# Three x tiles instead of two transposed on TensorE in the first stage of a gated mix of linear attention and GEGLU

## Chip, cores and metric

One core of one Trainium2 chip runs the kernel. The metric is the device time of one execution in microseconds (us), lower is better. A trace records one execution; its span, from the first instruction to the last, is about 1.25 us shorter than the time of the same execution.

## The reference

```python
# x: [1, 2048, 640]; 32 heads of 20; F = 1728; all bf16
g = sigmoid((x * gate_w).sum(-1, keepdims=True))
q, k, v = split(x @ wqkv)                          # [2048, 640] each
phi = lambda t: where(t > 0, t + 1, exp(t)) + 1e-6
kv  = einsum("bhsd,bhse->bhde", phi(k), v);  z = phi(k).sum over s
a   = (phi(q) @ kv) / (phi(q) . z + 1e-6) @ wo
b   = (gelu(x @ w_gate) * (x @ w_up)) @ w_down
out = g * a + (1 - g) * b
```

## The kernel before

The 2048 rows of x are 16 tiles of 128. For each tile, TensorE needs x transposed (five blocks of 128x128, one for each 128-row chunk `k` of the weights), multiplies it with the key and query columns of `wqkv`, and ScalarE and VectorE turn the sums in PSUM (the memory that TensorE's results go to, used here as eight banks, 0 to 7) into `phi(k)` and `phi(q)` ("phi" below). Loads are started on two queues, SP's and ACT's; a load "lands" when its data is there for the engines. Tiles 2 to 15 get their transpose from DMA and go through a per-tile loop, `KQ`. Tiles 0 and 1 are loaded plainly and transposed on TensorE, because that data is there sooner; they make up the first stage, which the change is about. In it, key products are made chunk by chunk as the chunks of the key weights land.

```python
NXN = 2                                   # tiles transposed on TensorE
load_x(0)                                 # SP queue unless "act" is given
load_wk(0)
load_x(1, "act")
load_wk(1)
load_wk(3)
load_wk(2, "act")
load_wk(4, "act")
# ... gate_w on ACT ...
load_wq(0, 2)                             # query weights, chunks 0-1
load_wq(2, KC, "act")                     # chunks 2-4
for i in range(NXN, NT):                  # DMA transposes, behind key chunk 4
    load_xT(i, after=([r_wk[4]] if i == NXN else ()))
# ...
SLOTS = [(0, 1), (2, 3), (4, 5), (6, 7)]  # PSUM banks of the n-th entry
seq = [("k", 0), ("k", 1), ("q", 0), ("q", 1)]
# KM(n, ks): key products of entry n, chunks ks;  QM(n, ks): query products
# T(i, ks, bank): transposes of tile i, then VectorE copies them to SBUF
# warm(count, n): filler matmuls of n columns on constants
warm(5, 512)
warm(1, 128)
T(0, [0], 7); T(0, [1, 2, 3, 4], 6)
warm(6, 128)
KM(0, [0])
T(1, [0], 7); T(1, [1, 2, 3, 4], 6)
warm(3, 128)
KM(1, [0])
for k in (1, 3):
    KM(0, [k]); KM(1, [k])
gate_col()
for k in (2, 4):
    KM(0, [k]); KM(1, [k])
# ... phi of the keys; QM of tiles 0 and 1 by chunk; phi of the queries ...
def KQ(i):
    b = 3 * (i % 2)                       # banks 0-2 or 3-5
    # ... 5 x (512 + 512 + 257 columns), then phi ...
for i in range(2, NT):
    KQ(i)
MGROUP = [((3, 4), (6, 7)), ((0, 1, 2), (3, 4, 5))]   # banks of the next stage
```

## Time and profile before

| | before |
|---|---|
| time, median of the first 3 runs (lowest to highest) | 274.45 us (274.27 to 275.06) |
| span of the trace | 273.2 us |
| TensorE busy | 269.7 us, 99% |
| first key matmul | 4.62 us |
| start of the per-tile loop (tile 2) | 11.40 us |
| from there to the start of the last matmul | 259.64 us |

The first part of the page of before: engine, busy time, share of the span, instructions.

```profile
PE 269.7 (99%) x1369; PEld 128.6 (47%) x1369; DVE 141.9 (52%) x251; ACT 76.0 (28%) x132; POOL 30.0 (11%) x28
```

TensorE (PE) is the limit. From 11.40 us on it has no gap of note, so the change can win only in the first 11 us. The timeline of PE there, for before; the columns are start, duration, engine, line of the kernel, operation, operands, count, and in brackets the idle time before and what ended it. L453 and L454 are one key chunk of one tile (512 and 128 columns), L433 the transposes, L419 the fillers, L540 the per-tile loop.

```profile
4.62 0.38 PE L453 MATMUL ps<-pool 128*128 128x512 bf16 x1 [0.18 <-DMA pool<-in_A_wqkv_dram]
4.84 0.22 PE L454 MATMUL ps<-pool 128*128 128x128 bf16 x1
4.89 0.44 PE L433 MATMUL ps<-pool 128*128 128x128 bf16 x5
5.17 0.34 PE L419 MATMUL ps<-const-bfloat16-1.0 128*128 128x128 bf16 x3
5.43 0.39 PE L453 MATMUL ps<-pool 128*128 128x512 bf16 x1
...
6.20 0.22 PE L454 MATMUL ps<-pool 128*128 128x128 bf16 x1
7.01 0.39 PE L453 MATMUL ps<-pool 128*128 128x512 bf16 x1 [0.59 <-DMA pool<-in_A_wqkv_dram]
...
11.40 0.38 PE L540 MATMUL ps<-pool 128*128 128x512 bf16 x1
```

Matmuls overlap, so the work is counted from start to start: 4.62 to 4.84 to 4.89 is 0.27 us for one key chunk of one tile; five transposes take 4.89 to 5.17, 0.28 us. After the matmul at 6.20 us TensorE stands still until key chunk 3 lands: 0.59 us after its modelled end, and 0.76 us more from start to start than without the wait. That is what the change goes for. The windows view of before, in the same stretch, ends with the DMA share and the rate:

```profile
core 0: us, PE busy (x) PEld busy (x) DVE busy (x) ACT busy (x) POOL busy (x), PEclk, DMA share, GB/s
5.00:6.00 1.00, 1.00 (x14) 0.67 (x12) 0.65 (x2) 0.00 (x0) 0.00 (x0) 1.00 1.02 302
6.00:7.00 1.00, 0.42 (x4) 0.08 (x2) 0.00 (x0) 0.00 (x0) 0.00 (x0) 1.00 0.94 308
```

The DMA engines are about full while TensorE waits (0.94 to 1.02), so I took it that in this trace the data could come in another order, but hardly sooner in total. The Trainium skill ("DMA: Bandwidth & Descriptors", Issuing engines are not separate DMA queues) says that copies issued by either engine run on the same 16 DMA engines and interleave. The landings agree: on SP, key chunks 0, 1 and 3 landed at 4.49, 5.46 and 6.96 us; on ACT, tile 1 of x and key chunks 2 and 4 at 4.68, 5.68 and 7.16. The column PEclk, the granted clock, reads 1.00 here.

### The profile page before, as it was taken

To read this page: it belongs to the slowest core of one execution; us is meant where nothing else is said; L and a number is where in the kernel's file an instruction comes from. 1 tells how busy PE (TensorE), PEld (TensorE's weight loads), DVE (VectorE), ACT (ScalarE), POOL (GpSimd) and SP (SyncE) were. 2 spreads that over 40 slices of the span, in tenths; PEclk is the share of its full clock that TensorE was granted. 3 is DMA by queue.
4 is the path that set the end of the run, shared out by engine and by line. 5 is a ranking of instruction groups with operands and counts; after the bars stand their busy time and mean duration, and the time that the engine had idled before them with its cause. 6 is when DMAs were issued, how large, how long until landed. Compare 5 with 4: busy or idle time off the path is not lost.

```text
span 273.2 us, 3449 instructions
## 1 busy us (share of the span) xinstructions
PE 269.7 (99%) x1369; PEld 128.6 (47%) x1369; DVE 141.9 (52%) x251; ACT 76.0 (28%) x132; POOL 30.0 (11%) x28
## 2 busy tenths in 40 slices
PE   7999999999999999999999999999999999999997
PEld 4555555544445444444444444444444444444444
DVE  2588989998234334999999999634210000000200
ACT  2355555310421454223222223224011121121021
POOL 5000000003240001242332422000000000000000
PEclk9999999999999999999999999999999999999999
DMA  6675999500300011522121221263031110110211
GB/s 207 179 118 122 322 402 386 143 3 12 65 19 2 23 49 51 182 45 48 26 48 24 48 42 34 60 215 109 5 77 38 41 38 19 38 41 19 58 58 41
DMA packets 42160, 23.61 MB, mean 86 GB/s; under 512 B 31519, under 2 KB 40735, under 8 KB 42015
## 3 DMA queue, kind: packets, MB, share of 16 engines
q1 hardware_dynamic: 41269, 22.40, 30.0%
q10 hardware_dynamic: 874, 0.98, 1.0%
q8 instruction: 11, 0.18, 0.3%
q14 instruction: 6, 0.05, 0.0%
HBM read 13.83 MB, written 2.63 MB: 60 GB/s over the span
## 4 chain that ended last, share of the span: by engine, by line
PE 97%; DMA 2%; SPq 0%; DVE 0%; issue 0%
PE ps L701 41%; PE ps L865 23%; PE ps L540 14%; PE ps L597 6%; PE ps L844 4%; DMA pool<-in_A_wqkv_dram 2%; PE ps L679 2%; PE ps L812 2%; PE ps L600 1%; PE ps L468 1%; PE ps L825 1%; PE ps L453 1%; PE ps L722 1%; PE ps L740 0%; SPq L340 0%; PE ps L469 0%
## 5 line engine op out<-in xcount | busy, mean ns | idle before, releaser
L701 PE MATMUL ps<-pool 128*128 128x512 bf16 x520 | 113.7, 379 | 0.0
L701 PEld LDWEIGHTS ps<-pool 128*128 128x128 bf16 x520 | 50.5, 98 | 60.0
L865 PE MATMUL ps<-pool 128*128 128x512 bf16 (+2 forms) x306 | 62.7, 367 | 0.0
L707 ACT ACTIVATE pool<-ps 128x512 f32<-128x512 f32 x52 | 31.0, 597 | 73.1 <-PE ps L701 73.1
L709 DVE TENSOR_TENSOR pool<-ps,pool 128x512 bf16<-128x512 f32 x52 | 34.7, 689 | 31.7 <-PE ps L701 30.4
L865 PEld LDWEIGHTS ps<-pool 128*128 128x128 bf16 x306 | 29.2, 98 | 33.4 <-issue 0.4
L540 PE MATMUL ps<-pool 128*128 128x512 bf16 (+1 forms) x210 | 38.1, 344 | 0.0
L848 DVE TENSOR_TENSOR pool<-ps,pool 128x512 bf16<-128x512 f32 x4 | 2.8, 692 | 61.5 <-PE ps L844 61.5
L755 POOL TENSOR_TENSOR pool<-pool 128x640 f32<-128x640 bf16 x16 | 22.5, 1406 | 72.9 <-DVE pool L757 66.2
L872 ACT ACTIVATE pool<-ps,pool 128x512 bf16<-128x512 f32 (+1 forms) x16 | 10.9, 681 | 68.6 <-PE ps L865 68.6
L540 PEld LDWEIGHTS ps<-pool 128*128 128x128 bf16 x210 | 20.5, 98 | 17.5
L559 DVE SCALAR_TENSOR_TENSOR pool<-ps,pool 128x128 bf16<-128x128 f32 (+2 forms) x42 | 25.3, 602 | 2.4
L550 ACT ACTIVATE pool<-ps 128x640 bf16<-128x640 f32 x28 | 19.7, 704 | 18.2 <-DVE pool L559 10.9
L597 PE MATMUL ps<-pool 128*128 128x512 bf16 x78 | 19.4, 379 | 0.0
L765 DVE TENSOR_TENSOR pool<-pool 128x640 bf16<-128x640 bf16 x16 | 13.2, 826 | 0.6
L763 DVE TENSOR_SCALAR pool<-pool 128x32 f32<-128x32 f32 x16 | 12.8, 802 | 0.6
L757 DVE TENSOR_REDUCE pool<-pool 128x32 f32<-128x640 f32 x16 | 12.9, 807 | 0.0
L645 DVE TENSOR_TENSOR pool<-pool 128x640 f32<-128x640 f32 x14 | 11.6, 825 | 0.5
L844 PE MATMUL ps<-pool 128*128 128x512 bf16 x52 | 11.6, 379 | 0.0
L647 POOL PARTITION_ALL_REDUCE pool<-pool x1 | 4.0, 3972 | 61.5 <-DVE pool L645 61.5
L597 PEld LDWEIGHTS ps<-pool 128*128 128x128 bf16 x78 | 7.0, 98 | 7.3
L556 DVE TENSOR_SCALAR pool<-pool 128x640 bf16<-128x640 bf16 x28 | 9.2, 327 | 1.8 <-ACT pool L550 0.3
(70 smaller groups left out, 105.8 us busy)
## 6 DMA issues: line engine op xcount, KB each, us to landing
out_dram<-pool SPq DMA_DIRECT2D x19, 128.0 KB, 1.7
pool<-in_B_w_gate_dram SPq DMA_DIRECT2D x1, 2080.0 KB, 13.8
pool<-in_B_w_up_dram SPq DMA_DIRECT2D x1, 2080.0 KB, 19.3
pool<-in_A_x_dram SPq DMA_DIRECT2D x1, 1280.0 KB, 8.6
pool<-in_B_w_down_dram SPq DMA_DIRECT2D x1, 1120.0 KB, 6.0
pool<-omg_row SPq DMA_DIRECT2D x1, 1024.0 KB, 4.8
pool<-in_A_x_dram SPq DMA_DIRECT2D x1, 960.0 KB, 5.7
pool<-in_A_wo_dram SPq DMA_DIRECT2D x6, 160.0 KB, 10.0
```

Of the source, the lines that this page charges most:

```text
L540: last = e.matmul(ps[:, b + p, 0:c1 - c0], xT[:, k, i * 128:(i + 1) * 128], wkq[:, k, c0:c1], start=(k == 0), stop=(k == KC - 1))
L550: P.op("act", lambda e: e.activation(e_buf[m], ps_flat[:, o:o + 640], ACT.Exp), reads=banks, writes=[r_e[m]])
L559: P.op("dve", lambda e, c0=c0, c1=c1: e.scalar_tensor_tensor(dst[:, c0:c1], ps_flat[:, o + c0:o + c1], 1.0 + EPS, e_buf[m][:, c0:c1], ALU. ...
L597: last = e.matmul(ps[:, b, :], pk[i][:, c * 128:(c + 1) * 128], x_aug[:, i, 0:512], start=(i == 0), stop=(i == NT - 1))
L701: last = e.matmul(ps[:, b, :], w[:, k, fc * 128:(fc + 1) * 128], xT[:, k, j * 512:(j + 1) * 512], start=(k == 0), stop=(k == KC - 1))
L707: P.op("act", lambda e: e.activation(ge[n], ps[:, gb, :], ACT.Gelu_apprx_tanh), reads=[bank[gb]], writes=[r_ge[n]])
L709: P.op("dve", lambda e: e.tensor_tensor(hT[fc][:, j * 512:(j + 1) * 512], ps[:, ub, :], ge[n], ALU.mult), reads=[bank[ub], r_ge[n]], write ...
L755: P.op("pool", lambda e: e.tensor_tensor(tmp[n], pq[i], z_b, ALU.mult), reads=[r_pq[i], r_zb], writes=[r_tmp[n]])
L757: P.op("dve", lambda e: e.tensor_reduce(den[n], tmp[n].rearrange("p (h d) -> p h d", h=32), AX.X, ALU.add), reads=[r_tmp[n]], writes=[r_de ...
L765: P.op("dve", lambda e: e.tensor_tensor(pq[i].rearrange("p (h d) -> p h d", h=32), pq[i].rearrange("p (h d) -> p h d", h=32), den[n].unsqu ...
L844: last = e.matmul(ps[:, b, :], wd[:, fc, 512:640], hT[fc][:, j * 512:(j + 1) * 512], start=False, stop=(fc == NFC - 2), skip_group_check=True)
L865: last = e.matmul(ps[:, pb, 0:c1 - c0], lhs, rhs, start=False, stop=(q == len(rows) - 1), skip_group_check=True)
```

## The change

The intent: while the key chunks land, give TensorE a third tile to work on, so that it has 0.81 us of work for each landed chunk instead of 0.54, and fill the wait. Tile 2 is loaded plainly, ahead of key chunk 2; keys of three tiles are made by chunk, then queries tile by tile. Six accumulations now share the four pairs of banks, so the queries of tiles 1 and 2 reuse the banks of the keys of tiles 0 and 1. The banks of the loop and of the next stage are shifted to fit.

```diff
-NXN = 2
+NXN = 3
@@ loads @@
+            load_wk(4)
+            load_x(2, "act")
             load_wk(2, "act")
-            load_wk(4, "act")
-            load_wq(0, 2)
-            load_wq(2, KC, "act")
+            for k in range(KC):
+                load_wq(k, ("act", "sp")[k % 2])
@@ first stage @@
-            seq = [("k", 0), ("k", 1), ("q", 0), ("q", 1)]
+            seq = [("k", 0), ("k", 1), ("k", 2), ("q", 0), ("q", 1), ("q", 2)]
             KM(1, [0])
-            (chunks 1, 3, gate, 2, 4 of tiles 0 and 1; phi; queries of both by chunk)
+            KM(0, [1])
+            KM(1, [1])
+            T(2, [0], 7)
+            T(2, [1, 2, 3, 4], 6)
+            KM(0, [2])
+            KM(1, [2])
+            for k in range(3):
+                KM(2, [k])
+            for n in range(3):
+                KM(n, [3])
             gate_col()
+            for n in range(3):
+                KM(n, [4])
+            for n in range(3):
+                phi1(n)
+                phi2(n)
+            for n in range(3, 6):
+                for k in range(KC):
+                    QM(n, [k])
+                phi1(n)
+                phi2(n)
@@ banks @@
-                b = 3 * (i % 2)
+                b = 4 * (i % 2)
-            for i in range(2, NT):
+            for i in range(NXN, NT):
-            MGROUP = [((3, 4), (6, 7)), ((0, 1, 2), (3, 4, 5))]
+            MGROUP = [((3, 4), (3, 7)), ((0, 1, 2), (4, 5, 6))]
```

(The first removed line in brackets stands for the old loop; the bulk load of x starts one tile later, by NXN.)

## The prediction

> # Prediction
>
> **What bounds the kernel now.** TensorE: the page's first part gives PE 269.7 us busy of a 273.2 us span (99%); the chain of waits is 97% PE. From 11.40 us (start of the per-tile stage, in the timeline) to the end the chain is matmuls without a gap, the granted clock 1.000. Only the first 11 us can give anything. There the timeline shows real matmuls from 4.62 us (key chunk 0 landed), a hole of 0.59 us before 7.01 us that ends on a wqkv DMA (key chunk 3, issued at 2.21 on SP, landing 4.8 us later), then dense work. The DMA engines are 0.8 to 1.08 busy from 2 to 8 us (the windows view). The Trainium skill ("DMA: Bandwidth & Descriptors", Issuing engines are not separate DMA queues) says that copies started by either engine run on the same 16 DMA engines and interleave; the trace agrees: the 160 KB key chunks 0 to 4, issued on SP and ACT, land at about 4.6, 5.4, 5.7, 7.0 and 7.1 us.
>
> **What the change does.** The projection work stays: 5 x 0.541 = 2.70 us a tile either way (0.270 us for a key chunk, start to start). Added: five transposes for tile 2, 0.28 us (as 4.89 to 5.17 us for tile 1); its 160 KB in ACT's queue ahead of key chunk 2; two VectorE copies (0.23 and 0.43 us). One DMA transpose goes, far from critical. Meant to be removed: the hole, about 0.75 us from the last start before it, filled with tile 2.
>
> **How much is critical.** Key chunk 2 moves to the place in ACT's queue where chunk 4 was, so I expect it at about 7.1 us (6.6 at best) instead of 5.7. All is unchanged to 6.24 us; tile 2's transposes run to 6.55; then PE waits about 0.5 us, because tile 2's chunks 0 and 1 are programmed behind tile 0's chunk 2. From 7.1: 11 key chunks and the gate column, 3.03 us, to 10.15; queries of tile 0 to 11.5. Queries of tile 1 go to banks 0-1, which the keys of tile 0 still hold: in before, VectorE's second operation on tile 0 ended at 10.52, 2.39 us after its last key chunk started at 8.13; now that chunk starts at about 9.35, so the banks come free at about 11.8: a new wait of 0.3 us. Queries of tiles 1 and 2, 2.7 us, end at 14.5.
>
> In before, tile 3 starts at 11.40 + 2.70 = 14.10 us. I expect 14.0 to 14.6, centre 14.4: about 0.75 us of hole removed, against 0.28 of transposes, 0.5 of a new hole and 0.3 of a bank wait. The rest is the same matmuls at the same rate: banks 0-2/4-6 are two sets as 0-2/3-5 were; 3 and 7 are free for the next stage as 6 and 7 were.
>
> **Time.** 274.45 + 0.2, so 274.6 us; 8 in 10 between 273.9 and 275.3 (before spread 274.27 to 275.06). Faster by over 2%: 0.01; within 2%: 0.98; slower by over 2%: 0.01. The full hole is only 0.3% of the time.
>
> **What would show the steps.** In PE's timeline: key chunk 2 of tile 0 starts near 7.1 us after about 0.5 us idle released by a wqkv DMA; queries of tile 1 wait about 0.3 us for VectorE; the per-tile loop starts at 14.0 to 14.6; PE's stretch from there to the end has before's length within 0.2 us.
>
> **What would make it wrong.** Chunk 2 landing near 6.5 us (a gain of 0.3 us); query weights landing after 10.2 us, or tile 3's DMA transpose after 14.4 (a loss of up to 1 us); a bank hand-over at the next stage that I misread; TensorE's clock falling back in the hole (it did not in before).

## The result, and the profile after

| | before | after | after, run again |
|---|---|---|---|
| median (lowest to highest), us | 274.40 (274.27 to 275.06), 4 runs | 275.12 (274.31 to 275.76), 4 runs | 274.72 (274.61 to 274.90), 6 runs |
| ratio to before, 95% interval | | 1.0023 [1.0001, 1.0046] | 1.0004 [0.9983, 1.0025] |
| span of the trace, us | 273.2 | 274.2 | 273.4 |

A ratio with its interval is from runs of the same rounds, and is not quite the ratio of the medians quoted; the before of the second comparison has a median of 274.43 (274.27 to 276.23, 11 runs). No gain shows: the two ratios lie 0.23% and 0.04% in the wrong direction, and the second interval includes a gain of up to 0.17%. (The second after is the unaltered kernel, run with the experiments.)

The first part of the page of after, and the timeline of PE in the stretch shown of before. L452 and L453 are a key chunk, L432 transposes, L418 fillers.

```profile
PE 269.2 (98%) x1353; PEld 129.3 (47%) x1379; DVE 142.1 (52%) x252; ACT 76.0 (28%) x132; POOL 30.0 (11%) x28
```

```profile
5.05 0.58 PE L452 MATMUL ps<-pool 128*128 128x512 bf16 x1 [0.66 <-DMA pool<-in_A_wqkv_dram]
5.43 0.31 PE L453 MATMUL ps<-pool 128*128 128x128 bf16 x1
5.54 0.74 PE L432 MATMUL ps<-pool 128*128 128x128 bf16 x5
6.07 0.53 PE L418 MATMUL ps<-const-bfloat16-1.0 128*128 128x128 bf16 x3
6.39 0.55 PE L452 MATMUL ps<-pool 128*128 128x512 bf16 x1
6.78 0.22 PE L453 MATMUL ps<-pool 128*128 128x128 bf16 x1
6.84 0.38 PE L452 MATMUL ps<-pool 128*128 128x512 bf16 x1
```

Two things differ, and neither is in the diff. Key chunk 0 landed at 4.92 us instead of 4.49, so the first key matmul is 0.43 us later. And every matmul up to about 6.7 us takes about twice as long: five transposes 0.53 us from start to start (5.54 to 6.07) instead of 0.28. The Trainium skill ("TensorE: Matmul & The Clock Gate", What's actually happening) describes a clock gate that starts at half rate and opens after enough activity, judged over a window of 3.4 us that runs free of the kernel, so that the moment differs from run to run. The steps in this trace fit it: consecutive matmuls of 128 columns start 107 ns apart before and 55 to 56 ns apart later. In before the rate rose between 4.21 and 4.62 us, just before the first key matmul; in this trace of after it rose at about 6.7. PEclk reads 1.00 throughout, so that row does not show it; the durations do. (The packed traces of before, warm_before and order_after also hold clock records, which no view prints: full rate from 4.21, 4.51 and 4.63 us on, for 269.65 us in all three, which is 79.0 of the skill's windows of 3.413 us. The other traces hold no record, and the row counts such time as 1.00.)

The predicted new wait shows further on. The timeline of PE in after where the queries of tile 0 end and those of tile 1 begin (L467 and L468 are a query chunk; L544 is the per-tile loop), and the line of the waits view that names it:

```profile
11.77 0.38 PE L467 MATMUL ps<-pool 128*128 128x512 bf16 x1
11.98 0.22 PE L468 MATMUL ps<-pool 128*128 128x129 bf16 x1
12.31 0.39 PE L467 MATMUL ps<-pool 128*128 128x512 bf16 x1
...
15.05 0.38 PE L544 MATMUL ps<-pool 128*128 128x512 bf16 x1
```

```profile
PEld ps L467 <- DVE pool L491: 0.4, 1, 0.4
```

From 11.98 to 12.31 is 0.33 us where 0.06 is usual: 0.27 us of waiting until VectorE (L491, the second operation of phi) has read banks 0 and 1. The per-tile loop starts with tile 3 at 15.05 us; before starts tile 3 at 11.40 + 2.70 = 14.10 us, so after is 0.95 us late there, the whole difference of the spans (1.0 us). From the start of tile 3 to the last matmul after takes 257.01 us and before 259.64 - 2.70 = 256.94 us.

### The profile page after: what moved, and what is told of

Same layout as the page of the kernel before. It is cut to its first block, busy times and chain, and to the rows that moved or that the text cites. A ratio compares the mean times of both kernels' runs of the same rounds, so it can differ in the third digit from the quotient of the medians.

```text
span 274.2 us, 3446 instructions
## 1 busy us (share of the span) xinstructions
PE 269.2 (98%) x1353; PEld 129.3 (47%) x1379; DVE 142.1 (52%) x252; ACT 76.0 (28%) x132; POOL 30.0 (11%) x28
## 4 chain that ended last, share of the span: by engine, by line
PE 96%; DMA 1%; issue 1%; DVE 1%; ACT 0%; SPq 0%
PE ps L705 41%; PE ps L869 23%; PE ps L544 13%; PE ps L601 6%; PE ps L848 4%; PE ps L816 2%; PE ps L683 2%; PE ps L604 1%; DMA pool<-in_A_wqkv_dram 1%; PE ps L452 1%; PE ps L467 1%; PE ps L829 1%; PE ps L726 1%; PE ps L744 0%; PE ps L453 0%
## 5 line engine op out<-in xcount | busy, mean ns | idle before, releaser
L705 PEld LDWEIGHTS ps<-pool 128*128 128x128 bf16 x520 | 50.5, 98 | 60.0
L869 PEld LDWEIGHTS ps<-pool 128*128 128x128 bf16 x306 | 29.1, 98 | 33.5 <-issue 0.4
L544 PE MATMUL ps<-pool 128*128 128x512 bf16 (+1 forms) x191 | 35.2, 343 | 0.2
L544 PEld LDWEIGHTS ps<-pool 128*128 128x128 bf16 x195 | 19.0, 98 | 16.2
L563 DVE SCALAR_TENSOR_TENSOR pool<-ps,pool 128x128 bf16<-128x128 f32 (+2 forms) x39 | 23.5, 603 | 2.2
L554 ACT ACTIVATE pool<-ps 128x640 bf16<-128x640 f32 x26 | 18.3, 704 | 17.2 <-DVE pool L563 9.8
L848 PE MATMUL ps<-pool 128*128 128x512 bf16 x50 | 11.3, 379 | 0.2 <-issue 0.2
L601 PEld LDWEIGHTS ps<-pool 128*128 128x128 bf16 x78 | 6.9, 98 | 7.2
L560 DVE TENSOR_SCALAR pool<-pool 128x640 bf16<-128x640 bf16 x26 | 8.5, 326 | 1.9 <-ACT pool L554 0.6
```

Source lines behind the costliest of these rows:

```text
L544: last = e.matmul(ps[:, b + p, 0:c1 - c0], xT[:, k, i * 128:(i + 1) * 128], wkq[:, k, c0:c1], start=(k == 0), stop=(k == KC - 1))
L554: P.op("act", lambda e: e.activation(e_buf[m], ps_flat[:, o:o + 640], ACT.Exp), reads=banks, writes=[r_e[m]])
L563: P.op("dve", lambda e, c0=c0, c1=c1: e.scalar_tensor_tensor(dst[:, c0:c1], ps_flat[:, o + c0:o + c1], 1.0 + EPS, e_buf[m][:, c0:c1], ALU. ...
L601: last = e.matmul(ps[:, b, :], pk[i][:, c * 128:(c + 1) * 128], x_aug[:, i, 0:512], start=(i == 0), stop=(i == NT - 1))
L705: last = e.matmul(ps[:, b, :], w[:, k, fc * 128:(fc + 1) * 128], xT[:, k, j * 512:(j + 1) * 512], start=(k == 0), stop=(k == KC - 1))
L848: last = e.matmul(ps[:, b, :], wd[:, fc, 512:640], hT[fc][:, j * 512:(j + 1) * 512], start=False, stop=(fc == NFC - 2), skip_group_check=True)
```

## The experiments

Theory at the outset: the change adds fixed work and a fixed wait on TensorE, and the landings limit the stage as before; the extra loss in the first trace of after comes from the late rise of the rate (A). Rivals: the idle time before key chunk 0 lets the rate fall (B), and tile 2's load delays the keys (C). A' is A with an addition: in before, a late rise is swallowed by the waits for landings that are there anyway.

All results in one table. "First key" and "tile 3" are starts in the trace; tile 3 of a version of before is the start of its loop plus 2.70. "Rate rises" is where the steps between matmuls change from the slow to the fast value. "Own work" is explained under the fifth experiment; "rest" is tile 3 minus first key minus own work, that is, what waits for landings and slow matmuls cost together. The 9.02 of order_after is an estimate, 9.30 less the bank wait of 0.28.

| kernel | median (range) of time, us | ratio to before [95%] | chunk 0 lands | first key | rate rises | own work | rest | tile 3 |
|---|---|---|---|---|---|---|---|---|
| before | 274.40 (274.27 to 275.06) | | 4.49 | 4.62 | 4.2 to 4.6 | 8.72 | 0.76 | 14.10 |
| after | 275.12 (274.31 to 275.76) | 1.0023 [1.0001, 1.0046] | 4.92 | 5.05 | 6.7 | 9.30 | 0.70 | 15.05 |
| after_again | 274.72 (274.61 to 274.90) | 1.0004 [0.9983, 1.0025] | 4.10 | 4.23 | 3.7 | 9.30 | 0.74 | 14.27 |
| warm_after | 275.15 (274.38 to 275.48) | 1.0015 [0.9994, 1.0037] | 4.42 | 5.16 | 6.7 | 9.30 | 0.65 | 15.11 |
| warm_before | 274.17 (274.03 to 274.87) | 0.9988 [0.9967, 1.0009] | 4.20 | 4.81 | 4.5 | 8.72 | 0.27 | 13.80 |
| order_after | 274.41 (274.21 to 274.66) | 0.9991 [0.9972, 1.0010] | 4.17 | 4.31 | 4.6 | 9.02 | 0.52 | 13.85 |
| banks_before | 274.33 (274.13 to 274.55) | 0.9996 [0.9984, 1.0008] | 4.24 | 4.38 | 5.8 | 8.72 | 1.15 | 14.25 |
| loads_before | 274.25 (273.98 to 274.33) | 0.9991 [0.9980, 1.0003] | 4.15 | 4.29 | 5.5 | 8.72 | 1.01 | 14.02 |
| swap_after | 274.35 (273.93 to 274.84) | 0.9994 [0.9979, 1.0009] | 4.70 | 4.83 | 6.1 | | | 14.34 |
| swap_nofill | 274.75 (274.17 to 274.93) | 1.0006 [0.9995, 1.0018] | 4.24 | 4.37 | 5.9 | | | 14.39 |
| cold_before | 274.98 (274.64 to 276.09) | 1.0030 [1.0014, 1.0047] | 4.32 | 4.46 | 6.9 | | | 14.68 |
| cold_after | 275.44 (275.03 to 276.11) | 1.0041 [1.0028, 1.0054] | 4.38 | 4.51 | 7.3 | | | 15.05 |

The two kernels with one look each (late_before, late_after) follow in the text.

### 1. The changed kernel again

No edit.

> The changed kernel unaltered, for a second trace and for its spread. Theory A (phase of the clock): TensorE's rate doubles at a moment that differs from run to run; in the profile of before it had risen by 4.6 us, in the profile of after only at about 6.6 us, which cost about 0.7 us. Then the runs spread again over about 274.3 to 275.8, and in this trace the first key matmuls are at 0.38 us with the per-tile loop starting at 14.0 to 14.4, or at 0.58 us with a start near 15. Theory B (the idle 0.66 us before key chunk 0 lets the rate fall): slow first matmuls appear if and only if that idle is longer than about 0.5 us. Theory C (loads): chunk 0 lands at 4.9 us or later in every trace of after, because of tile 2's load, and the time stays at 275.1 or above. Common to all: the wait of the queries of tile 1 for VectorE is 0.27 us again.

Measured: 274.72 us, with a spread of only 0.3 us. The timeline of PE, same stretch:

```profile
4.23 0.38 PE L452 MATMUL ps<-pool 128*128 128x512 bf16 x1
4.45 0.22 PE L453 MATMUL ps<-pool 128*128 128x128 bf16 x1
4.50 0.44 PE L432 MATMUL ps<-pool 128*128 128x128 bf16 x5
...
5.26 0.22 PE L453 MATMUL ps<-pool 128*128 128x128 bf16 x1
5.57 0.39 PE L452 MATMUL ps<-pool 128*128 128x512 bf16 x1
...
6.07 0.22 PE L453 MATMUL ps<-pool 128*128 128x128 bf16 x1
6.30 0.45 PE L432 MATMUL ps<-pool 128*128 128x128 bf16 x5
6.87 0.39 PE L452 MATMUL ps<-pool 128*128 128x512 bf16 x1
...
14.27 0.59 PE L544 MATMUL ps<-pool 128*128 128x512 bf16 x2
```

The same program in another execution: chunk 0 landed at 4.10 us, the rate had risen at 3.7, five transposes take 0.28 us. Now TensorE waits for landings instead: 5.26 to 5.57 (key chunk 1, 0.25 us more than the usual 0.06), 6.07 to 6.30 (tile 2 of x, 0.18), and 0.28 after the last transpose of tile 2 until key chunk 2, landed at 6.83. That is the predicted pattern, with the 0.5 us spread over three waits of 0.71 us in all. The loop starts at 14.27 us, inside the predicted 14.0 to 14.6. The bank wait is there again (11.21 to 11.53, 0.27 more than usual). Theory C is out as a fixed cost: tile 2's load was issued at 1.78 us in both traces of after, and chunk 0 landed at 4.92 in one and 4.10 in the other. The expected wide spread of the times did not appear in these six runs.

### 2. More fillers before key chunk 0, in after and in before

```diff
-            warm(6, 128)
+            warm(14, 128)
```

> After, with 14 instead of 6 filler matmuls behind the transposes of tile 0, so that TensorE is busy until about 4.9 us. Theory B: the rate is high from 4.6 us on in all runs, spread below 0.4 us, median about 274.4 to 274.6. Theory A: the fillers change nothing, spread about 1 us as in after, some first key matmuls still at 0.58 us; median about 275. Theory C: as A, with chunk 0 landing late.

> Before, with the same 14 fillers. Theory B: 274.3 to 274.5, spread below 0.4 us, the 275.06 of before no longer seen. Theory A: spread as in before (274.3 to 275.1), ratio to before within 0.1%.

Measured: 275.15 us (274.38 to 275.48) and 274.17 us (274.03 to 274.87). The timeline of PE of the changed kernel with more fillers:

```profile
3.67 1.70 PE L418 MATMUL ps<-const-bfloat16-1.0 128*128 128x128 bf16 x14
5.16 0.63 PE L452 MATMUL ps<-pool 128*128 128x512 bf16 x1
5.59 0.31 PE L453 MATMUL ps<-pool 128*128 128x128 bf16 x1
5.69 0.74 PE L432 MATMUL ps<-pool 128*128 128x128 bf16 x5
```

By the profile TensorE has had no idle time from its first filler on, and its matmuls are still slow until about 6.7 us. Theory B falls: the rate does not fall in a short idle stretch, it has not yet risen. Theory A holds in this trace, and the spread of 1.1 us over the runs is what it expects. (B falls by the first trace of after alone, too: its matmuls ahead of the idle stretch already start 107 ns apart.) In before with the same fillers the rate rose at 4.5 us, the time is not told from before's, and the spread stayed (0.84 us). No earlier rise is seen from more activity ahead of the work: over the twelve traces with fillers from 0.8 us on (the two late kernels of experiment 5 included), it came at 3.7, 4.2 to 4.6, 4.5, 4.6, 4.7, 5.5, 5.8, 5.9, 6.1, 6.5, 6.7 and 6.7 us. That is spread over 3.0 us, which agrees with the skill's free-running window of 3.4 us. The four traces with the longer fillers (warm and late) lie at 4.5, 4.7, 6.5 and 6.7, no earlier than the rest.

### 3. Keys finished tile by tile

```diff
             for n in range(3):
                 KM(n, [3])
-            gate_col()
-            for n in range(3):
                 KM(n, [4])
+                if n == 1:
+                    gate_col()
```

> After, with key chunks 3 and 4 done tile by tile instead of chunk by chunk, so that the banks of tile 0's keys are handed over two chunks earlier. If the wait of 0.27 us in front of the queries of tile 1 is what I take it for (VectorE reading banks 0 and 1), it is gone (under 0.05 us), and the per-tile loop starts 0.27 us earlier than in after at equal start of the first key matmul and equal rate; the median of the time about 0.2 to 0.3 us under that of after_again, if the spread allows it to be seen. If the wait comes from something else (query weights, the gate column), it stays.

Measured: 274.41 us against 274.72 of the unaltered kernel in the same rounds. The timeline of PE at the start of the queries of tile 1 (11.12):

```profile
10.85 0.38 PE L467 MATMUL ps<-pool 128*128 128x512 bf16 x1
11.06 0.22 PE L468 MATMUL ps<-pool 128*128 128x129 bf16 x1
11.12 0.38 PE L467 MATMUL ps<-pool 128*128 128x512 bf16 x1
```

The wait is gone (0.06 us from 11.06 to 11.12). So it was the bank hand-over, and it was an accident of order: with the last key chunk of tile 0 two places earlier, and that of tile 1 one place, the banks are free in time. The gain of 0.31 us in the medians agrees with the 0.27 us; the intervals of the ratios overlap.

### 4. Banks alone, loads alone

Before with only the new banks, and before with only the new loads (tile 2 of x early on ACT and left out of the bulk load, key chunk 4 on SP, query weights by chunk):

```diff
-                b = 3 * (i % 2)
+                b = 4 * (i % 2)
-            MGROUP = [((3, 4), (6, 7)), ((0, 1, 2), (3, 4, 5))]
+            MGROUP = [((3, 4), (3, 7)), ((0, 1, 2), (4, 5, 6))]
```

```diff
+            load_wk(4)
+            load_x(2, "act")
             load_wk(2, "act")
-            load_wk(4, "act")
-            load_wq(0, 2)
-            load_wq(2, KC, "act")
+            for k in range(KC):
+                load_wq(k, ("act", "sp")[k % 2])
-            dma_in(x_aug[:, NXN:8, 0:640], ...)
+            dma_in(x_aug[:, 3:8, 0:640], ...)
```

> Before with the new banks alone (0-2 and 4-6 for the per-tile loop, 3 and 7 for the next stage). Expected neutral: ratio to before within 0.1%, median 274.3 to 274.5. From the start of the per-tile loop to the last matmul before took 259.64 us in both of its traces; after took 0.07 us more than its share (one tile of 2.70 us less). If the banks cause that, 259.7 here; if not, 259.64. It also serves as another trace of before's first stage: if TensorE's rate rises late here (near 6.6 us), theory A' says that the hole in front of key chunk 3 swallows the loss, so the per-tile loop still starts at 11.3 to 11.5 us; a rival (late rise costs before as much as after) says 12.0 or more.

> Before with after's loads alone: tile 2 of x loaded early on ACT ahead of key chunk 2, chunk 4 on SP, query weights by chunk on both queues; TensorE's program, tile order and banks as in before. If tile 2's load delays the keys, chunk 2 lands near 6.9 instead of 5.7 us and chunk 4 near 7.4 instead of 7.1, the last landed key still ends the wait near 7.0, and the per-tile loop starts at 11.3 to 11.7: time within 0.1% of before (274.3 to 274.7). If the loads are the main cost of the change, 274.9 or more.

Measured: 274.33 and 274.25 us, neither told apart from before. The banks are neutral: from the start of the loop to the last matmul 259.63 us, as in before, so the 0.07 us that after takes more there is not theirs; where it comes from is open beyond the trace's hint (at the start of the next stage one matmul starts 0.07 us late, its bank freed late by VectorE). The loads alone cost nothing either: chunk 2 did move to 7.00 us as expected and chunk 4 to 7.41, and the loop still started at 11.32. So C is out for the median too.

Both traces also bear on the rate. It rose at 5.8 and 5.5 us, so that 0.6 to 0.7 us was lost to slow matmuls (an estimate: half of the time from the first key matmul to the rise), yet tile 3 starts at 14.25 and 14.02 us, around the 14.10 of before's early rise. The timeline of PE of before with the new loads shows why:

```profile
4.29 0.63 PE L452 MATMUL ps<-pool 128*128 128x512 bf16 x1
...
6.36 0.22 PE L453 MATMUL ps<-pool 128*128 128x128 bf16 x1
6.86 0.39 PE L452 MATMUL ps<-pool 128*128 128x512 bf16 x1 [0.28 <-DMA pool<-in_A_wqkv_dram]
```

In this trace the slow start only used up part of the wait for the next chunk, which landed at 6.81 us. So in before, the idle time that the change set out to fill also serves as a cushion for a late rise. The expected start for the banks version, 11.3 to 11.5 us, was missed by 0.05 us: its key chunks landed early (chunk 3 at 6.04) and the first query chunk late (8.69), so it waited there instead.

### 5. All loads landed and the rate high before the stage begins

In both kernels:

```diff
-            warm(5, 512)
+            warm(37, 512)
```

> Before with 37 instead of 5 wide filler matmuls ahead of everything, so that all loads have landed and the rate is high before the first transpose. Only TensorE's own work and its hand-overs are left. From the first key matmul to the start of tile 3 (start of the per-tile loop plus 2.70 us) I expect 8.6 to 8.7 us: 20 chunks of 0.27, the transposes, 3 fillers and copies' wait of tile 1 0.55, and 2.70.

> After with the same 37 fillers. From the first key matmul to the start of the per-tile loop (tile 3): if the fixed cost of the change on TensorE is the transposes of tile 2 (0.28 us) and the bank wait (0.27 us), 9.15 to 9.25 us, 0.55 us more than late_before. If the difference between the two kernels came only from landings and from the rate, they agree within 0.1 us.

Measured (one look each, times 280.50 and 282.02 us, which mean nothing by themselves since the fillers last until the rate has risen at 4.7 or 6.5 us and run on from there): from the first key matmul to the start of the loop 11.45 to 17.47, plus 2.70 for tile 2, is 8.72 us in before; 12.35 to 21.65 is 9.30 us in after. The lines of the timeline of PE of before with long fillers, first key matmul and start of the loop, and then of after, with the bank wait between them:

```profile
11.45 0.38 PE L453 MATMUL ps<-pool 128*128 128x512 bf16 x1
...
17.47 2.10 PE L540 MATMUL ps<-pool 128*128 128x512 bf16 x9
```

```profile
12.35 0.38 PE L452 MATMUL ps<-pool 128*128 128x512 bf16 x1
...
18.58 0.22 PE L468 MATMUL ps<-pool 128*128 128x129 bf16 x1
18.91 0.39 PE L467 MATMUL ps<-pool 128*128 128x512 bf16 x1
...
21.65 0.59 PE L544 MATMUL ps<-pool 128*128 128x512 bf16 x2
```

This is the "own work" of the table: products, transposes and hand-overs, without landings and without the slow rate. Both came out 0.02 to 0.05 us above what I expected; the difference, 0.58 us, is the fixed cost of the change: 0.28 us of transposes, 0.28 us of bank wait (18.58 to 18.91), 0.02 us unexplained. The idea that the kernels differ only by landings and rate (0.1 us) is out.

With this, the column "rest" can be read: 0.76 us in before, 0.70 and 0.74 in after. In neither trace of the unaltered after is it clearly smaller than in the one trace of before. In after_again it is waits for landings (0.71), in the first trace slow matmuls: 5.05 to 6.74 us at half rate is, as an estimate, 0.85 us lost, somewhat less since TensorE would have waited for VectorE's copy in it anyway.

### 6. Tile 2 loaded behind key chunk 2, work in landing order

```diff
-            load_x(2, "act")
             load_wk(2, "act")
+            load_x(2, "act")
...
-            T(2, ...); KM(0, [2]); KM(1, [2]); KM(2, [0]), [1], [2]
-            KM(0..2, [3]); gate_col(); KM(0..2, [4])
+            for k in (2, 3):
+                KM(0, [k]); KM(1, [k])
+            T(2, [0], 7); T(2, [1, 2, 3, 4], 6)
+            KM(0, [4]); KM(1, [4]); gate_col()
+            for k in range(KC):
+                KM(2, [k])
```

(the program's lines are shortened here), and the same without the three fillers before `KM(1, [0])`:

> After with tile 2 loaded behind key chunk 2 instead of ahead of it, and TensorE's work in the order of landing: tiles 0 and 1 take chunks 0 to 3, then tile 2 is transposed, tiles 0 and 1 take chunk 4, tile 2 takes all its chunks, then the queries. If the waits of after are those of its two orders (tile 2 ahead of chunk 2: idle time before chunk 2; tile 0's keys finished late: 0.27 us for banks 0 and 1), both go: key chunk 2 lands at about 5.6, the per-tile loop starts at 13.4 to 13.6 us when the rate rises by 4.6 us, and up to 0.9 us later when it rises at 6.6. Median 273.8 to 274.3, below before by 0.1 to 0.6 us. Rival (the load of tile 2 itself delays all chunks): it starts at 13.9 or later even with an early rise, and the time is not below before.

> The version with tile 2 loaded behind chunk 2 and with work in landing order, now without the 3 fillers between the transposes of tile 1 and its first key chunk. With a late rise these cost 0.32 us, with an early one about 0.1 us that the wait for VectorE's copy takes instead. Median 274.0 to 274.3, a little under swap_after (274.35), the slow end (274.84) coming down by about 0.3. If the fillers help the rate to rise, no gain or a loss.

Measured: 274.35 us (273.93 to 274.84), just above the expected range, and 274.75 us (274.17 to 274.93) without the fillers. In the trace of the first, the waits for landings and banks are gone: after key chunk 0 TensorE is never held up by either. But its rate rose at 6.1 us and chunk 0 landed at 4.70, so the loop started at 14.34 us, as expected for a late rise. An early rise was expected to give 13.4 to 13.6; no trace caught one. The fastest single run, 273.93, is 0.20 us under the fastest of before in those rounds, and the time is not told apart from before's (median 274.48 in those rounds). Taking the three fillers out, expected to help, gave a median 0.4 us higher, though in other rounds and on another chip; in its trace chunk 1 landed at 6.41 us (5.58 with the fillers), which cost a wait of about 0.5 us. Landings vary that much between executions, so I do not put this down to the fillers; it stays open.

### 7. No fillers before the first transposes

In both kernels:

```diff
-            warm(5, 512)
-            warm(1, 128)
```

> Before without the six fillers ahead of the transposes of tile 0. TensorE is idle until about 3.1 us, so its rate should rise later, somewhere from 6.5 to 9.5 us (it rose from 3.7 to 6.7 with activity from 0.8 us). Until then its work runs at half rate. Theory A': before waits for landings anyway, so the first 0.75 us or so of that loss is swallowed: with a rise at 7 us the per-tile loop starts at about 11.6, at 9 us at about 12.5. Time 274.7 to 275.8.

> After without the same six fillers. Theory A': after has more to do on TensorE in that time and less waiting to swallow the loss, so it loses more than cold_before: the ratio of cold_after to cold_before is larger than that of after to before (1.0004 to 1.0023): 0.6 to 1.4 us slower than cold_before, time 275.8 to 276.8. Rival (the rate's rise is not what separates after from before): the distance stays at 0.3 us or so.

Measured: 274.98 and 275.44 us. Before is slower than with fillers, by 0.6 us (against 274.37 in the same rounds); after was not run with fillers in these rounds, and lies 0.3 and 0.7 us above its two earlier medians (275.12 and 274.72). So in before the fillers earn their place. The distance between them, 0.46 us in the medians, lies between what theory A' expected (0.6 to 1.4) and the rival (0.3): it decides nothing (cold_after itself came in under the expected 275.8 to 276.8). The rates rose at 6.9 and 7.3 us, later than in any of the twelve traces with fillers from 0.8 us on, and in before chunk 1 landed only at 6.68 us, so its trace mixes both causes (tile 3 at 14.68 us against 15.05).

## Why the prediction was right or wrong

The range held and the kernel is "within 2%" as forecast. The class was safe, since the whole wait is 0.3% of the time. The range was not: two of the first four runs of after (275.41 and 275.76) lie above it, and eight of all ten in it, as "8 in 10" says, but partly by draws that the prediction did not reckon with. Point by point:

- "The full hole is only 0.3% of the time", and TensorE is the limit from 11.40 us on: right. From tile 3 on the two kernels agree within 0.07 us (predicted: 0.2).
- Five transposes, 0.28 us: right (13.98 to 14.26 us in late_after). A bank wait of 0.3 us for the queries of tile 1: right (0.27 in both traces of after and 0.28 in late_after, gone in order_after). Together they are the fixed cost of 0.58 us (late_before and late_after).
- "PE waits about 0.5 us" before key chunk 2, which lands "at about 7.1 us": half right. In after_again chunk 2 landed at 6.83, and the wait was 0.28 there, with 0.25 and 0.18 in front of chunk 1 and tile 2 of x, which I had not expected. In the first trace of after it did not occur, because TensorE was 1.1 us late by then.
- "I expect 14.0 to 14.6" for the start of tile 3: right in after_again (14.27), and by the predicted path: from key chunk 2 on 7.4 us were predicted (7.1 to 14.5) and 7.40 measured (6.87 to 14.27). It was wrong in the first trace (15.05). The step that failed there is "All is unchanged to 6.24 us". I took 4.62 us and the fast rate from one trace as properties of the program. They are properties of an execution: chunk 0 landed at 4.10 to 4.92 us and the rate rose at 3.7 to 6.7 us, whatever the kernel. "TensorE's clock falling back in the hole" was on my list of risks, but that is not what happens: with no idle time at all it was still slow (warm_after).
- The size: I predicted +0.2 us. The medians say +0.7 us in the first comparison and +0.3 in the second, with intervals that reach from -0.17% to +0.46%. The size is not settled better than that.

Where did the expected gain go? The wait that the change aimed at was not removed but turned into others: the sum of landing waits and slow matmuls is 0.70 to 0.74 us in after and 0.76 us in before, while 0.58 us of fixed work and waiting came on top. That sum can't be read as a law: it ranges from 0.27 to 1.15 us over the versions of before. The wait aimed at is itself a draw: with before's loads, key chunk 3 landed at 6.04, 6.14, 6.59, 6.96 and 7.54 us in five executions (banks_before, late_before, warm_before, before, cold_before).

The two traced executions of after (275.41 and 274.67 us) differ in the rise (6.7 and 3.7 us), but also in the landing of chunk 0 (4.92 and 4.10), so the traces alone don't part the two. An estimate from their numbers: with the landings of the first trace and the fast rate, TensorE would have come to key chunk 2 at about 6.97 us instead of 7.66, and to tile 3, 7.4 us later, at 14.4 instead of 15.05; the late rise then cost 0.7 of the 0.78 us between them. With chunk 0 at 4.10 and the rise at 6.7 the same sum gives 14.6, so that the rise alone would have cost 0.4. For the runs without a trace the cause of the spread is only argued, and the spread itself is not sure to be after's own: the six later runs of after span 0.29 us, and the eleven of before in the same rounds 1.96. What stays open: no trace of before with its fillers caught a rise later than 5.8 us, so how much of a rise at 6.7 us before would swallow is not shown.

## What to carry to other kernels

Work that fills a wait at the start pays only if it is cheaper than the wait and does not put off what the wait was for: here the filler brought its own transposes, its own load in front of an awaited chunk, and a hand-over of banks, 0.58 us in all for the transposes and the hand-over, against a wait of 0.76 us that then came back in other places. Before pricing a start-up stage to a tenth of a microsecond, look at several executions of it; one trace gives one draw of the landings and of the rise of TensorE's rate. Where accumulators are reused, finish the one that must be handed over first first: in the trace of order_after that alone won the 0.27 us back.

## What the Trainium skill lacked or had wrong

- "TensorE: Matmul & The Clock Gate", Part 4: PE-mode transpose, says that the full rate "doesn't engage" for transposes. Here transposes of 128x128 start 106 to 107 ns apart before the rise and 55 to 56 ns apart after it, like other matmuls (0.53 against 0.28 us for five). Whether transposes alone would bring the rise about is not shown here.
- The same page puts the moment of the rise at "around 4µs into sustained matmul activity, ±500ns run-to-run" (What you observe). With activity from 0.82 us, it came at 3.7 to 6.7 us over twelve traces, 2.9 to 5.9 us into it (3.7, 3.8, 5.7 and 5.9 in the warm and late traces, by the profile without a gap before the rise). The free window described further on in the page fits this width, the ±500 ns does not; and the earliest rise, 2.9 us in, comes before a whole window of 3.4 us of activity.
- No page that I read says how much a first load's landing varies between executions: key chunk 0 landed at 4.10 to 4.92 us after being issued at 1.25 to 1.27, and chunk 1 at 5.24 to 6.68.
